# Decay-attention and two feed-forward blocks on one core: input blocks as one 112-row transfer, values on two queues, other planner constants

## The chip, the cores and the metric

One core of a Trainium2 chip runs the whole program. The metric is device time in microseconds; lower is better. The engines are TensorE (PE, with its weight loads PEld), VectorE (DVE), ScalarE (ACT), GpSimd (POOL) and SyncE (SP). TensorE's clock is granted at one of two levels, 2.4 GHz (1.00 in the profile) or 1.2 GHz (0.50).

## The reference

Batch 4, 8 heads, 768 steps, head dimension 48; the 3072 rows of 384 that come out go through two feed-forward blocks.

```python
for t in range(S):                       # attention with a decaying state
    cur = u * k[t] outer v[t]
    y[t] = r[t] @ (state + cur)
    state = w[t] * state + k[t] outer v[t]
x = y as (3072, 384)
x = ((x @ w1) * (x @ w2)) @ w3 @ w_out              # 384 -> 1024 -> 1024 -> 384
out = max(x @ v1, x @ v2, x @ v3) @ v_out           # 384 -> 768 -> 384
```

The weights arrive as 64-bit floats and are converted on the chip.

## The kernel before

**Tiling.** The sequence of each pair of heads is cut into units of 384 steps (`T`), each of six chunks of 64 (`NC`, `C`). There are eight units (`NU`) and in each unit four tiles j (`NJ`) of two heads; the two heads of a tile stand at partitions 0 to 47 and 64 to 111 (`PR` = 112).

**Attention of a unit** (`plan_unit`). For each tile, SyncE loads the block `dm` (L303): decays, reversed keys, receptances, 1159 floats a row. It is loaded in two halves of 48 rows; the rows between them are set once by six memsets in `att_tiles` (L258 to L261). VectorE makes two scans over it, `sf` (L345) and `e` (L352); GpSimd makes the scaled keys `kk` (L356) and receptances `x1`, `x2` (L370, L372). From a second block `tok` (L312) GpSimd makes r*k*u (L314, L316), whose sums per step are the diagonal, `diag`: on ScalarE for unit 1 (L327, `DIAG_ACT`), on VectorE for the others (L329). TensorE makes query-key products (L392), transposes (L398) and chunk states (L459); the states are chained over the chunks by `chain` (L475, L476), on GpSimd for units 0 and 1 (`ON_POOL`), on VectorE for the others. The output product `y` (L417) uses values that were loaded in two halves to `TA` and `TB` (L445, L446). ScalarE and VectorE copy it out as two parts (`yh` L427, `yl` L428), and `xp` (L435) moves a part of it to other partitions by DMA.

**Weights.** Blocks of `wo` (3), `w3` (8) and `w12` (8) are loaded (L758) and converted by VectorE in three passes (L784, L787, L790). W = w3 @ w_out is multiplied out once on TensorE (L826): block i needs w3's block i and all of `wo`. `w12` is split into high and low parts (L817, L818).

**Feed-forward.** For each unit and each of eight slices, A (L509 into `rot`), its product with VectorE (L852), a split (L854, L856), and B with W. After all units, the second feed-forward block runs over the eight units and writes the output.

**The order.** `Plan` holds every step with its engine, cost, needs, claims of buffers and due time. `schedule` runs a list schedule over that model and issues the steps in the resulting order; each engine, and each queue of DMA issues, then runs its steps in that order. A step's urgency is its latest start, worked back from due times. DMAs are modelled as one stream: bytes over `RATE`, plus `LAND`. The due times come from `T_A` (first A), `UNIT` (length of a unit), `T_W` and `D_W` (product of W's block i: T_W + D_W * i), `LEAD` (how far ahead of its first A a unit's attention is due) and `T_V`. Steps with `lock` keep VectorE and GpSimd apart in the model.

```python
add(("dm", *k), "SP", 1.0, load, after=last, size=96 * DMW * 4, ...)
add(("wmul", i, q), "PE", 2.73, w_mul, ..., due=self.T_W + self.D_W * (i + 0.5 * q))
self.due = {"x": lambda u: tA(u * FT) - (min(self.LEAD[1] + self.LEAD[2] * (u - 1), self.LEAD[3]) if u else self.LEAD[0])}
```

Of the kernel before, what the change touches and what calls it, by code (L numbers as in the profile page):

```python
# [9 lines left out]
F32 = mybir.dt.float32  # L10
# [11 lines left out]
B, H, S, D = 4, 8, 768, 48  # L22
NU = 8
T = 384
C = 64
NC = T // C
NJ = 4
DM, FF, FF2 = 384, 1024, 768
KT, FT, MT = DM // 128, FF // 128, FF2 // 128
PR = 112  # L30
NW = NC * (C + 1) + 1
O_K, O_R = NW, NW + T
DMW = NW + 2 * T
# [14 lines left out]
class Plan:  # L48
# [162 lines left out]
class Net:  # L211
# [4 lines left out]
    def constants(self, pool):  # L216
        nc = self.nc
        self.first = pool.tile([PR, NC, C + 1], F32, name="first")
        nc.vector.memset(self.first, 0.0)
        nc.vector.memset(self.first[:, :, 0:1], 1.0)  # L220
        self.inv = [pool.tile([PR, NC, C + 1], F32, name=f"inv{i}") for i in range(2)]
        for t in self.inv:
            nc.gpsimd.memset(t, 0.0)
        self.ident = pool.tile([128, 128], F32, name="ident")
        nc.gpsimd.memset(self.ident, 0.0)
        nc.gpsimd.affine_select(out=self.ident, in_=self.ident, pattern=[[-1, 128]], base=0,
                                channel_multiplier=1, compare_op=ALU.not_equal, fill=1.0)
# [12 lines left out]
        self.wjunk = pool.tile([PR, NW + 1], BF16, name="wjunk")  # L240
        self.il = pool.tile([PR, NU, NJ, NC], F32, name="il")
        self.ub = pool.tile([128, NJ, D], F32, name="ub")

    def att_tiles(self):

        nc, t = self.nc, lambda name, shape, n=1, dt=F32: [self.ap.tile(shape, dt, name=f"{name}{i}") for i in range(n)]
        self.dm, self.tok = t("dm", [PR, DMW], 2), t("tok", [128, 2, NC, D], 2)
        self.e, self.sf = t("e", [PR, NC, C + 1], 2), t("sf", [PR, NC, C + 1], 2)
        self.kk = t("kk", [PR, T], 2)
        self.x1, self.x2 = t("x1", [PR, NC, C], self.NX), t("x2", [128, NC, C], self.NX)  # L250
        self.kt, (self.y,) = t("kt", [128, NC // 2, PR], 2), t("y", [PR, 2, T], 1, F32R)
        self.cd = t("c", [128, NC], 2)
        self.V2, = t("V2", [128, NC // 2, NJ, 2 * D])
        self.TA, = t("TA", [PR, NC * NJ * D])
        self.TB, = t("TB", [128, NC * NJ * D])
        self.U, = t("U", [PR, NC, NJ, D])
        self.fin, = t("fin", [PR, NJ, D])
        for dm in self.dm:  # L258
            nc.vector.memset(dm[32:64, 0:O_K], 1.0)
            nc.vector.memset(dm[32:64, 0:O_K - 1].rearrange("p (c t) -> p c t", t=C + 1)[:, :, 0:1], 0.0)  # L260
            nc.vector.memset(dm[32:64, O_K - 1:], 0.0)  # L261

    NX = 4
    DIAG_ACT = (1,)

    ON_POOL = {"chain": (0, 1), "l": ()}

    def on(self, what, u, dve, pool):
        return ("POOL", pool) if u in self.ON_POOL[what] else ("DVE", dve)
# [4 lines left out]
    def plan_unit(self, u):  # L274

        nc, a, P = self.nc, self.a, self.plan
# [8 lines left out]
        for j in range(NJ):  # L285
# [3 lines left out]
            def dm(k=k):  # L289
                return self.dm[slot["dm", *k][0]]  # L290
# [7 lines left out]
            def bwd(k=k):  # L298
                return dm(k)[0:PR, O_K - 1:0:-1]

            def load(k=k):
                for h in (0, 1):
                    nc.sync.dma_start(dm(k)[64 * h:64 * h + D], a["dm"][k[0], k[1], D * h:D * h + D])  # L303

            add(("dm", *k), "SP", 1.0, load, after=last, size=96 * DMW * 4,
                claims=[("dm", [(w, *k) for w in ("sf", "e", "x1", "x2", "kk", "wchk0", "wchk1")])])
            lt = [("tok", u, j - 1)] if j else [("tok", u - 1, NJ - 1)] if u else []

            def tok(k=k):
                return self.tok[slot["tok", *k][0]]  # L310

            add(("tok", *k), "SP", 0.55, lambda k=k: nc.sync.dma_start(tok(k), a["tok"][k]), after=lt,  # L312
                size=128 * 2 * NC * D * 4, claims=[("tok", [("diag", *k)])])
            add(("rk", *k), "POOL", 0.80, lambda k=k: G.tensor_mul(tok(k)[:, 0], tok(k)[:, 0], tok(k)[:, 1]),  # L314
                [("tok", *k)], lock=True)
            add(("rku", *k), "POOL", 0.80, lambda k=k: G.tensor_mul(  # L316
                tok(k)[:, 0], tok(k)[:, 0], self.ub[:, k[1], :].unsqueeze(1).to_broadcast([128, NC, D])),
                [("rk", *k)], lock=True)

            def cd(k=k):  # L320
                return self.cd[slot["diag", *k][0]]

            def diag(k=k):
                if k[0] in self.DIAG_ACT:
                    for c in range(NC):
                        t = tok(k)[:, 0, c]
                        SC.activation(out=t, in_=t, func=AF.Copy, accum_out=cd(k)[:, c:c + 1])  # L327
                else:
                    V.tensor_reduce(out=cd(k), in_=tok(k)[:, 0], axis=AX.X, op=ALU.add)  # L329

            add(("diag", *k), *(("ACT", 1.6) if u in self.DIAG_ACT else ("DVE", 0.45)), diag,
                [("rku", *k)], claims=[("c", [("dg0", *k), ("dg1", *k)])])

            def sf(k=k):
                return self.sf[slot["sf", *k][0]]
# [28 lines left out]
                return self.x2[slot["x2", *k][0]]  # L364

            def r(k, p, q):
                return dm(k)[p:q, O_R:].rearrange("p (c t) -> p c t", t=C)
# [57 lines left out]
            add(("y", *k), "PE", 0.5, y, [("v1", u), ("s0", u, 0), ("s0", u, 1), *[("s1", u, i) for i in range(4)], ("qk0", *k), ("qk1", *k)] +  # L425
                ([("Ab", 8 * u - 9)] * (u > 1) if j < KT else [("xp", u - 1, j)] * (u > 0)), claims=[("ab", [("yl", *k)])], kind="s")
            add(("yh", *k), "ACT", 0.48, lambda k=k, yt=yt: SC.copy(yt(0), bank(("y", *k))[0:PR, 0:T]), [("y", *k)])  # L427
            add(("yl", *k), "DVE", 0.555, lambda k=k, yt=yt: V.tensor_sub(yt(1), bank(("y", *k))[0:PR, 0:T], f32(yt(0))),  # L428
# [599 lines left out]
def layout(inputs):  # L1028
# [7 lines left out]
    we = np.zeros((NU, NJ, 2, D, NC * (C + 1) + 1), np.float32)
    kd = np.zeros((NU, NJ, 2, D, NC, C), np.float32)
    rd = np.zeros((NU, NJ, 2, D, NC, C), np.float32)
    for i, h in enumerate((1, 0)):
        def rows(x):  # L1040
            return x[:, :, h].transpose(0, 1, 4, 2, 3)
        we[:, :, i, :, :-1].reshape(NU, NJ, D, NC, C + 1)[..., 1:] = rows(W)
        kd[:, :, i] = rows(K)[..., ::-1, ::-1]
        rd[:, :, i] = rows(R)
    dm = np.concatenate([x.reshape(NU, NJ, 2 * D, -1) for x in (we, kd, rd)], axis=3)
# [19 lines left out]
    res |= {"dm": dm, "tok": tok, "v1": v1, "v2": v2, "u": ub, "w3": w3, "wo": wo, "w12": w12}  # L1065
# [21 lines left out]
```

## Time and profile before

| | |
|---|---|
| Median of 3 runs | 771.3 us (770.09 to 771.99) |
| Profiled execution, its own time | 770.51 us |
| Its span, first to last instruction | 768.7 us |
| Mean granted TensorE clock | 0.983 |
| Busy: PE, DVE, ACT, POOL | 737.4, 447.0, 332.9, 243.5 us |

The time of the profiled execution is 1.8 us more than its span. Durations below come from this one execution. A busy TensorE at the low clock level does half the work, so busy time and granted clock are read together. A group's line number is that of the kernel; the feed-forward products have one line, that of a helper (L509).

### The profile page before, as it was taken

To read this page: it belongs to the slowest core of one execution; us is meant where nothing else is said; L and a number is where in the kernel's file an instruction comes from. 1 tells how busy PE (TensorE), PEld (TensorE's weight loads), DVE (VectorE), ACT (ScalarE), POOL (GpSimd) and SP (SyncE) were. 2 spreads that over 40 slices of the span, in tenths; PEclk is the share of its full clock that TensorE was granted. 3 is DMA by queue.
4 is the path that set the end of the run, shared out by engine and by line. 5 is a ranking of instruction groups with operands and counts; after the bars stand their busy time and mean duration, and the time that the engine had idled before them with its cause. 6 is when DMAs were issued, how large, how long until landed. Compare 5 with 4: busy or idle time off the path is not lost.

```text
span 768.7 us, 14960 instructions
## 1 busy us (share of the span) xinstructions
PE 737.4 (96%) x5994; PEld 696.9 (91%) x5994; DVE 447.0 (58%) x731; ACT 332.9 (43%) x798; POOL 243.5 (32%) x293
## 2 busy tenths in 40 slices
PE   3499999999999999999999999999999999999996
PEld 1366788999999999999999999999999999999996
DVE  7798999677876777585547887323232323232222
ACT  2244556354635445354343335667766422222211
POOL 4484678655575565545002332000000000000000
PEclk8689999999999999999999999999999999999999
DMA  7988753445354543344024447576767200000001
GB/s 252 308 274 251 218 185 85 109 110 151 98 139 126 126 93 111 92 125 93 2 82 172 129 159 280 197 256 204 245 204 242 76 32 1 32 1 32 1 31 35
DMA packets 30588, 102.94 MB, mean 134 GB/s; under 512 B 4272, under 2 KB 7472, under 8 KB 30512
## 3 DMA queue, kind: packets, MB, share of 16 engines
q1 hardware_dynamic: 30368, 101.72, 43.2%
q8 instruction: 49, 0.80, 0.4%
q14 instruction: 27, 0.22, 0.1%
q10 hardware_dynamic: 144, 0.20, 0.1%
HBM read 91.28 MB, written 8.26 MB: 129 GB/s over the span
## 4 chain that ended last, share of the span: by engine, by line
PE 93%; DVE 5%; issue 1%; POOL 1%; DMA 0%; ACT 0%; SPq 0%; DVEq 0%; POOLq 0%
PE bank L509 40%; PE rot L509 38%; PE bank L826 6%; PE bank L417 3%; PE bank L392 2%; PE bank L459 1%; PE bank L398 1%; PE bank L393 1%; DVE conv L784 1%; DVE x L405 1%; DMA dm<-in_dm 0%; DVE conv L787 0%; DVE e L352 0%; POOL w L818 0%; DVE gs L856 0%
## 5 line engine op out<-in xcount | busy, mean ns | idle before, releaser
L509 PE MATMUL rot<-xT,w 128*128 128x384 f32 x1152 | 217.2, 339 | 0.9 <-POOL w L818 0.7
L509 PEld LDWEIGHTS rot<-xT,w 128*128 128x128 f32 x1152 | 198.6, 188 | 4.3 <-POOL w L818 1.3
L509 PE MATMUL bank<-x2s,v 128*128 128x384 f32 x684 | 125.6, 336 | 0.0
L509 PEld LDWEIGHTS bank<-x2s,v 128*128 128x128 f32 x684 | 119.0, 188 | 0.0
L509 PE MATMUL bank<-gs,W 128*128 128x384 f32 x576 | 112.6, 338 | 1.2 <-DVE gs L856 1.2
L509 PEld LDWEIGHTS bank<-gs,W 128*128 128x128 f32 x576 | 100.7, 188 | 2.5 <-DVE gs L856 1.8
L956 DVE TENSOR_TENSOR m<-m,bank 128x384 f32<-128x384 f32 x58 | 32.1, 554 | 109.2 <-PE bank L509 99.9
L509 PE MATMUL bank<-vo,ms 128*128 128x384 f32 x432 | 83.5, 337 | 0.0
L509 PE MATMUL rot<-x2s,v 128*128 128x384 f32 x450 | 83.5, 336 | 0.0
L509 PEld LDWEIGHTS rot<-x2s,v 128*128 128x128 f32 x450 | 78.4, 188 | 0.0
L509 PEld LDWEIGHTS bank<-vo,ms 128*128 128x128 f32 x432 | 76.5, 187 | 0.2 <-DVE ms L963 0.2
L961 ACT CAST ms<-m 128x384 fp32r<-128x384 f32 x48 | 24.6, 513 | 96.7 <-DVE m L956 96.4
L850 ACT COPY a<-rot 128x384 f32<-128x384 f32 x64 | 30.6, 478 | 77.6 <-PE rot L509 77.4
L956 DVE TENSOR_TENSOR m<-m,rot 128x384 f32<-128x384 f32 x38 | 21.0, 554 | 66.9 <-PE rot L509 61.0
L854 ACT CAST gs<-g 128x384 fp32r<-128x384 f32 x64 | 32.9, 515 | 61.9 <-DVE g L852 60.3
L852 DVE TENSOR_TENSOR g<-a,rot 128x384 f32<-128x384 f32 x64 | 35.3, 551 | 41.4 <-PE rot L509 40.9
L356 POOL TENSOR_TENSOR kk<-dm,sf 112x384 f32<-112x384 f32 x32 | 32.0, 1006 | 62.3 <-PE bank L393 26.7
L405 DVE COPY_PREDICATED x<-later,bank 64x384 f32<-64x384 uint32 x64 | 37.9, 592 | 22.8 <-PE bank L393 21.8
L826 PE MATMUL bank<-wo,piece 128*128 128x384 f32 x128 | 46.9, 525 | 3.4 <-DVE piece L790 3.4
L856 DVE TENSOR_TENSOR gs<-g,gs 128x384 fp32r<-128x384 f32 x64 | 41.0, 642 | 15.0 <-ACT gs L854 14.8
L370 POOL TENSOR_TENSOR x<-dm,e 48x384 f32<-48x384 f32 x32 | 30.9, 966 | 44.5 <-DVE e L352 27.1
L826 PEld LDWEIGHTS bank<-wo,piece 128*128 128x128 f32 x128 | 25.7, 206 | 21.0 <-DVE piece L790 3.5
(117 smaller groups left out, 1080.1 us busy)
## 6 DMA issues: line engine op xcount, KB each, us to landing
dm<-in_dm SPq DMA_DIRECT2D x64, 217.3 KB, 4.1
tok<-in_tok SPq DMA_DIRECT2D x32, 288.0 KB, 4.0
wst<-in_w SPq DMA_DIRECT2D x8, 1024.0 KB, 8.7
top<-in_w SPq DMA_DIRECT2D x8, 1024.0 KB, 5.0
vst<-in_moe_w SPq DMA_DIRECT2D x9, 768.0 KB, 4.7
top<-in_moe_w SPq DMA_DIRECT2D x9, 768.0 KB, 4.4
wst<-in_w SPq DMA_DIRECT2D x8, 768.0 KB, 5.2
top<-in_w SPq DMA_DIRECT2D x8, 768.0 KB, 4.2
```

The costliest lines, as they stand in the source:

```text
L356: add(("kk", *k), "POOL", 0.86, lambda k=k: G.tensor_mul(kk(k).rearrange("p (c t) -> p c t", t=C), dm(k)[0:PR, O_K:O_R].rearrange("p (c t) ...
L370: add(("x1", *k), "POOL", 0.94, lambda k=k: G.tensor_mul(x1(k)[64:PR], r(k, 64, PR), e(k)[64:PR, :, 0:C]), [("e", *k)], after=lx, lock=Tru ...
L405: add((f"qk{i}", *k), "DVE", 0.59, lambda k=k, x=x, p=p: V.copy_predicated(x(k)[p:p + 64], self.later.bitcast(U32)[p:p + 64].unsqueeze(1). ...
L417: nc.tensor.matmul(ps[0:48, s], self.TA[:, o], x1(k)[:, c, :], start=True, stop=True)
L509: r = self.nc.tensor.matmul(ps, w[p], x[q], start=first and i == 0, stop=last and i == 2)
L826: nc.tensor.matmul(ps[:, 0:DM], t[:, jt * 128:(jt + 1) * 128], wo[:, jt * DM:jt * DM + DM], start=jt == 0, stop=jt == FT - 1)
L850: add(("a", g), "ACT", 0.48, lambda g=g: SC.copy(at[slot["a", g][0]], rot[slot["Aa", g][0]][:, 0:T]), [("Aa", g)], claims=[("a", [("m", g)])])
L852: add(("m", g), "DVE", 0.555, lambda g=g: V.tensor_mul(gt[slot["m", g][0]], at[slot["a", g][0]], rot[slot["Ab", g][0]][:, 0:T]), [("a", g) ...
L854: add(("h", g), "ACT", 0.51, lambda g=g: SC.copy(gst[slot["h", g][0]][:, 0], gt[slot["m", g][0]]), [("m", g)], claims=[("gs", [("B", g)])])
L856: add(("l", g), *self.on("l", u, 0.56, 0.95), lambda g=g, u=u: self.eng("l", u).tensor_sub(gst[slot["h", g][0]][:, 1], gt[slot["m", g][0]] ...
L956: V.tensor_max(t, t, p)
L961: add(("mh", h), "ACT", 0.51, lambda h=h: SC.copy(p2["ms"][slot["mh", h][0]][:, 0], p2["m1"][slot["mx", h, 0][0]]), [("mx", h, 2)], claims ...
```

## The change

The block `dm` becomes one transfer of 112 rows: its rows are padded to 1184 floats, and the rows between the two heads come from memory with it (ones and zeros laid out by the host), so the six memsets go. Of the values, `TA` stays on SyncE's queue and `TB` goes to ScalarE's. The table `ub` (and a small new one, `uf`, which nothing reads with the constants given) is loaded through ScalarE's queue. The diagonal of unit 1 moves from ScalarE to VectorE (the new branch for TensorE is switched off: `DIAG_PE` is empty). The chain of unit 1 moves from GpSimd to VectorE, those of units 3 and 5 from VectorE to GpSimd. The planner gets other constants, and its order follows from them.

```diff
-DMW = NW + 2 * T
+DMW = (NW + 2 * T + 31) // 32 * 32
-    RATE = 285e3
-    LAND = 3.0
+    RATE = 390e3
+    LAND = 2.4
-        for dm in self.dm:
-            nc.vector.memset(dm[32:64, 0:O_K], 1.0)
-            nc.vector.memset(dm[32:64, 0:O_K - 1].rearrange("p (c t) -> p c t", t=C + 1)[:, :, 0:1], 0.0)
-            nc.vector.memset(dm[32:64, O_K - 1:], 0.0)
-    DIAG_ACT = (1,)
-    ON_POOL = {"chain": (0, 1), "l": ()}
+    DIAG_PE = ()
+    ON_POOL = {"chain": (0, 3, 5), "l": ()}
-            def load(k=k):
-                for h in (0, 1):
-                    nc.sync.dma_start(dm(k)[64 * h:64 * h + D], a["dm"][k[0], k[1], D * h:D * h + D])
-            add(("dm", *k), "SP", 1.0, load, after=last, size=96 * DMW * 4, ...)
+            add(("dm", *k), "SP", 0.5, lambda k=k: nc.sync.dma_start(dm(k), a["dm"][k]), after=last, size=128 * DMW * 4, ...)
-                add(("xp", *k), "SP", 2.6, xp, ..., size=96 * 2 * T * 4)
+                add(("xp", *k), "SP", 3.7, xp, ..., size=128 * 2 * T * 4)
-        def v1():
-            nc.sync.dma_start(self.TA[0:64], a["v1"][u, 0:64])
-            nc.sync.dma_start(self.TB[64:128], a["v1"][u, 64:128])
-        add(("v1", u), "SP", 1.1, v1, [("y", u - 1, j) for j in range(NJ)] if u else [], size=128 * NC * NJ * D * 4)
+        for i, (t, p, queue) in enumerate(((self.TA, 0, nc.sync), (self.TB, 64, nc.scalar))):
+            add(("v1", u, i), ("SP", "ACT")[i], 0.55, lambda t=t, p=p, queue=queue: queue.dma_start(t[p:p + 64], a["v1"][u, p:p + 64]),
+                [("y", u - 1, j) for j in range(NJ)] if u else [], size=64 * NC * NJ * D * 4)
-    T_A, UNIT, T_W, D_W, LEAD, T_V = 29.5, 37.7, 18.9, 2.0, (1.0, 16.9, 3.6, 35.2), 20.0
+    T_A, UNIT, T_W, D_W, LEAD, T_V = 22.2, 34.6, 11.0, 5.2, (0, 15.4, 5.1, 35.2), 19.0
-        nc.sync.dma_start(self.ub, a["u"])
+        nc.scalar.dma_start(self.uf, a["uf"])
+        nc.scalar.dma_start(self.ub, a["u"])
```

## Rows read from the trace of the kernel before

**Rows 1.** The page: TensorE's busy time and share; its busy tenths in 40 slices.

```profile
PE 737.4 (96%) x5994; PEld 696.9 (91%) x5994; DVE 447.0 (58%) x731; ACT 332.9 (43%) x798; POOL 243.5 (32%) x293
PE   3499999999999999999999999999999999999996
```

**Rows 2.** Stretches: length, busy time by engine (instructions), granted clock, DMA share, GB/s.

```profile
0.00:40.00 40.00, 17.24 (x127) 10.11 (x128) 30.65 (x42) 9.54 (x27) 19.21 (x32) 0.73 0.91 276
...
80.00:134.00 54.00, 52.09 (x561) 46.12 (x560) 50.75 (x91) 30.43 (x80) 41.15 (x50) 1.00 0.52 155
134.00:760.00 626.00, 625.31 (x5001) 613.94 (x5001) 327.87 (x555) 275.26 (x619) 157.24 (x175) 1.00 0.38 115
```

**Rows 3.** TensorE's waits: whom for, us in total, times, longest.

```profile
PE bank L398 <- POOL kk L356: 11.1, 3, 5.4
PE bank L459 <- DMA V<-in_v: 4.8, 1, 4.8
```

**Rows 4.** Timeline of the start: start us, us, engine, line, operation, count.

```profile
0.82 0.40 SPq L743 DMA_DIRECT2D ub<-in_u  x1
...
3.38 0.70 DVE L261 MEMSET dm<- 32x769 f32 x1
...
4.11 2.12 SPq L303 DMA_DIRECT2D dm<-in_dm  x4
...
8.43 0.97 DVE L345 TENSOR_TENSOR_SCAN sf<-dm,first 112x390 f32<-112x390 f32 x1 [3.01 <-DMA dm<-in_dm]
```

**Rows 5.** Stretches in which halves, weight blocks, and halves again are loaded.

```profile
4.50:8.30 3.80, 3.78 (x6) 1.24 (x4) 0.76 (x2) 0.00 (x0) 0.00 (x0) 1.00 0.87 198
...
11.00:20.00 9.00, 0.83 (x4) 0.50 (x4) 8.69 (x10) 2.40 (x10) 5.52 (x5) 0.54 1.02 407
21.50:26.00 4.50, 1.12 (x3) 0.79 (x3) 4.01 (x5) 0.70 (x2) 3.03 (x6) 0.50 1.03 207
```

**Rows 6.** DMA issues before 20 us: size of each, median us to landing.

```profile
dm<-in_dm SPq DMA_DIRECT2D x7, 217.3 KB, 4.9
...
TA<-in_v SPq DMA_DIRECT2D x1, 288.0 KB, 13.3
```

**Rows 7.** Timeline of VectorE: two instructions after idle time.

```profile
26.88 0.97 DVE L345 TENSOR_TENSOR_SCAN sf<-dm,first 112x390 f32<-112x390 f32 x1 [1.30 <-DMA dm<-in_dm]
...
30.67 1.20 DVE L405 COPY_PREDICATED x<-later,bank 64x384 f32<-64x384 uint32 x2 [2.59 <-PE bank L393]
```

**Rows 8.** W's blocks: timelines of TensorE and VectorE, and the chain's longest piece.

```profile
24.91 4.76 PE L826 MATMUL bank<-wo,piece 128*128 128x384 f32 x8 [3.38 <-DVE piece L790]
...
50.92 5.43 PE L826 MATMUL bank<-wo,piece 128*128 128x384 f32 x16
...
75.94 1.20 DVE L784 TENSOR_SCALAR conv<-wst 128x1024 uint32<-128x1024 uint32 x1
...
78.50 1.22 DVE L790 SCALAR_TENSOR_TENSOR piece<-wst,conv 128x1024 uint32<-128x1024 uint32 x1
...
65.29 20.84 PE bank L826 x64
```

**Rows 9.** Diagonals and chain steps on VectorE (ns min/median/max); scans during unit 1's chain (us, mean ns).

```profile
L329 DVE TENSOR_REDUCE c<-tok x28: 417/447/455, 24.8 to 351.7; 128x6 f32<-128x288 f32 x28
...
L475 DVE TENSOR_TENSOR U<-U,il x30: 333/359/897, 159.9 to 385.9; 112x192 f32<-112x192 f32 x30
...
L476 DVE TENSOR_TENSOR U<-U x30: 357/358/851, 160.2 to 386.3; 112x192 f32<-112x192 f32 x30
...
L345 DVE TENSOR_TENSOR_SCAN sf<-dm,first 112x390 f32<-112x390 f32 x2 | 4.3, 2139 | 0.0
```

**Rows 10.** SyncE's queue, its own waits: us in total, times, longest.

```profile
SPq L445 <- PE bank L418: 23.5, 7, 7.7
```

More of the change, by code (lines that the diff above doesn't have):

```diff
@@ L242, in constants @@
         self.ub = pool.tile([128, NJ, D], F32, name="ub")
+        self.uf = pool.tile([PR, NJ], F32, name="uf")
     def att_tiles(self):
@@ L299, in bwd @@
                 return dm(k)[0:PR, O_K - 1:0:-1]
-            def load(k=k):
-                for h in (0, 1):
-                    nc.sync.dma_start(dm(k)[64 * h:64 * h + D], a["dm"][k[0], k[1], D * h:D * h + D])
-            add(("dm", *k), "SP", 1.0, load, after=last, size=96 * DMW * 4,
-                claims=[("dm", [(w, *k) for w in ("sf", "e", "x1", "x2", "kk", "wchk0", "wchk1")])])
-            lt = [("tok", u, j - 1)] if j else [("tok", u - 1, NJ - 1)] if u else []
+            add(("dm", *k), "SP", 0.5, lambda k=k: nc.sync.dma_start(dm(k), a["dm"][k]), after=last, size=128 * DMW * 4,
+                claims=[("dm", [(w, *k) for w in ("sf", "e", "x1", "x2", "kk", "wchk0", "wchk1") + ("rk",) * (u in self.DIAG_PE)])])
@@ L309, in tok, with first @@
+            def first(u):
+                return "rk" if u in self.DIAG_PE else "tok"
+            lt = [(first(u), u, j - 1)] if j else [(first(u - 1), u - 1, NJ - 1)] if u else []
             def tok(k=k):
                 return self.tok[slot["tok", *k][0]]
[L312 to L315, printed above, removed]
@@ L316, in plan_unit @@
-            add(("rku", *k), "POOL", 0.80, lambda k=k: G.tensor_mul(
-                tok(k)[:, 0], tok(k)[:, 0], self.ub[:, k[1], :].unsqueeze(1).to_broadcast([128, NC, D])),
-                [("rk", *k)], lock=True)
             def cd(k=k):
                 return self.cd[slot["diag", *k][0]]
-            def diag(k=k):
-                if k[0] in self.DIAG_ACT:
-                    for c in range(NC):
[L326 to L329, printed above, removed]
@@ L331, in plan_unit, with rk, dp @@
-            add(("diag", *k), *(("ACT", 1.6) if u in self.DIAG_ACT else ("DVE", 0.45)), diag,
-                [("rku", *k)], claims=[("c", [("dg0", *k), ("dg1", *k)])])
+            if u in self.DIAG_PE:
+                def rk(k=k):
+                    return self.tok[slot["rk", *k][0]].rearrange("p a c d -> p (a c d)")[0:PR, 0:T]
+                add(("rk", *k), "POOL", 0.95, lambda k=k: G.tensor_mul(
+                    rk(k), dm(k)[0:PR, O_K:O_R], dm(k)[0:PR, O_R + T - 1:O_R - 1:-1]), [("dm", *k)], after=lt, lock=True,
+                    claims=[("tok", [("dp", *k)])])
+                def dp(k=k):
+                    ps = self.ab[slot["dp", *k][0]]
+                    for c in range(NC):
+                        q = slice(T - c * C - C, T - c * C)
+                        nc.tensor.matmul(ps[0:64, c:c + 1], rk(k)[64:PR, q], self.uf[64:PR, k[1]:k[1] + 1], start=True, stop=True)
+                        nc.tensor.matmul(ps[64:128, c:c + 1], rk(k)[0:48, q], self.uf[0:48, k[1]:k[1] + 1], start=True, stop=True)
+                add(("dp", *k), "PE", 0.35, dp, [("rk", *k)], claims=[("ab", [("diag", *k)])], kind="s")
+                add(("diag", *k), "ACT", 0.2, lambda k=k: SC.copy(cd(k), self.ab[slot["dp", *k][0]][:, 0:NC]), [("dp", *k)],
+                    claims=[("c", [("dg0", *k), ("dg1", *k)])])
+            else:
+                add(("tok", *k), "SP", 0.55, lambda k=k: nc.sync.dma_start(tok(k), a["tok"][k]), after=lt,
+                    size=128 * 2 * NC * D * 4, claims=[("tok", [("diag", *k)])])
+                add(("rk", *k), "POOL", 0.80, lambda k=k: G.tensor_mul(tok(k)[:, 0], tok(k)[:, 0], tok(k)[:, 1]),
+                    [("tok", *k)], lock=True)
+                add(("rku", *k), "POOL", 0.80, lambda k=k: G.tensor_mul(
+                    tok(k)[:, 0], tok(k)[:, 0], self.ub[:, k[1], :].unsqueeze(1).to_broadcast([128, NC, D])),
+                    [("rk", *k)], lock=True)
+                add(("diag", *k), "DVE", 0.45, lambda k=k: V.tensor_reduce(out=cd(k), in_=tok(k)[:, 0], axis=AX.X, op=ALU.add),
+                    [("rku", *k)], claims=[("c", [("dg0", *k), ("dg1", *k)])])
@@ L366, in r @@
             def r(k, p, q):
-                return dm(k)[p:q, O_R:].rearrange("p (c t) -> p c t", t=C)
+                return dm(k)[p:q, O_R:O_R + T].rearrange("p (c t) -> p c t", t=C)
             lx = [("x1", u, j - 1)] if j else [("x1", u - 1, NJ - 1)] if u else []
@@ L423, in yt @@
                 return t[:, i]
-            add(("y", *k), "PE", 0.5, y, [("v1", u), ("s0", u, 0), ("s0", u, 1), *[("s1", u, i) for i in range(4)], ("qk0", *k), ("qk1", *k)] +
+            add(("y", *k), "PE", 0.5, y, [("v1", u, 0), ("v1", u, 1), ("s0", u, 0), ("s0", u, 1), *[("s1", u, i) for i in range(4)], ("qk0", *k), ("qk1", *k)] +
                 ([("Ab", 8 * u - 9)] * (u > 1) if j < KT else [("xp", u - 1, j)] * (u > 0)), claims=[("ab", [("yl", *k)])], kind="s")
@@ L437, in plan_unit @@
             if j == KT:
-                add(("xp", *k), "SP", 2.6, xp, [("yl", u, i) for i in range(NJ)] + [("Ab", 8 * u - 9)] * (u > 1), size=96 * 2 * T * 4)
+                add(("xp", *k), "SP", 3.7, xp, [("yl", u, i) for i in range(NJ)] + [("Ab", 8 * u - 9)] * (u > 1), size=128 * 2 * T * 4)
         nd = NJ * D
@@ L1034, in layout @@
     R, K, V, W = units(r), units(k), units(v), units(w)
[L1036 to L1039, printed above, removed]
+    dm = np.zeros((NU, NJ, PR, DMW), np.float32)
+    we = dm[..., 0:O_K - 1].reshape(NU, NJ, PR, NC, C + 1)
+    we[..., 1:] = 1
+    kd, rd = (np.zeros((NU, NJ, PR, NC, C), np.float32) for _ in range(2))
+    for h, p in ((1, 0), (0, 64)):
         def rows(x):
             return x[:, :, h].transpose(0, 1, 4, 2, 3)
[L1042 to L1045, printed above, removed]
+        we[:, :, p:p + D, :, 1:] = rows(W)
+        kd[:, :, p:p + D] = rows(K)[..., ::-1, ::-1]
+        rd[:, :, p:p + D] = rows(R)
+    dm[..., 0:O_K - 1] = we.reshape(NU, NJ, PR, -1)
+    dm[..., O_K:O_R] = kd.reshape(NU, NJ, PR, -1)
+    dm[..., O_R:O_R + T] = rd.reshape(NU, NJ, PR, -1)
+    uf = np.zeros((PR, NJ), np.float32)
+    for h, p in ((1, 0), (0, 64)):
+        uf[p:p + D] = u.reshape(NJ, 2, D)[:, h].T
     tok = np.stack([R[:, :, :, :, ::-1], K[:, :, :, :, ::-1]], axis=2)
@@ L1064, in layout @@
     res["u2"] = u2
-    res |= {"dm": dm, "tok": tok, "v1": v1, "v2": v2, "u": ub, "w3": w3, "wo": wo, "w12": w12}
+    res |= {"dm": dm, "tok": tok, "v1": v1, "v2": v2, "u": ub, "w3": w3, "wo": wo, "w12": w12, "uf": uf}
     for n in ("moe_w1", "moe_w2", "moe2_w1", "moe2_w2", "moe2_w3", "moe2_w_out"):
```

## The prediction

> **What bounds the kernel now.** I first read the busy shares and the forty slices. TensorE is busy 96% of the span, and the only slices under nine tenths are the first two and the last [rows 1]. Nearly all that can be won lies in the first 40 us; the last slice is the drain of the output, which the change doesn't touch.
>
> Next, four stretches. In the first 40 us TensorE works 17.24 us, so it idles 22.8 us, and at a mean granted clock of 0.73; VectorE works 30.65 us of the 40 and the DMA engines are busy 0.91 of them. From 80 to 134 us TensorE idles 1.9 us and VectorE works 50.75 of 54. From 134 to 760 us TensorE idles 0.7 us of 626 [rows 2]. So past 134 us the time is a sum of matmuls that no edit changes; the span is that sum plus whatever TensorE lost before.
>
> Who makes it lose? Its waits name the key products (GpSimd) and the state values (a DMA) [rows 3], but those wait for VectorE and the transfers themselves. The W blocks show how tight it is: the three passes that convert the last w3 block run on VectorE from 75.94 to 79.72 us, and TensorE's last four products of W run without a break from 65.29 to 86.13 us at some 5.4 us a block [rows 8], so the last starts near 80.7, 1 us after its block is converted. TensorE looks full from 40 us on, but it is fed just in time. VectorE's work up to about 134 us is the bound, and each microsecond by which it runs earlier is one off the span.
>
> **The change part by part.**
>
> *Memsets and the first block.* Before, SyncE's first issue is the table of u at 0.82 us; the first block of decays, keys and receptances is issued at 4.11 us, right after the memset of its tile ends (3.38 + 0.70), and the first scan starts at 8.43 us [rows 4]. After, no memset writes that tile and u's table is on ScalarE's queue, so the block is SyncE's first issue, at about 0.82: 3.3 us earlier. VectorE has nothing but memsets in those 6 us, and the removed memsets themselves sit inside that wait, so they count nothing beyond it. ScalarE has no instruction before 8.43 us, so its two small issues cost it nothing; without that cover they would cost some 0.4 us each, like u's issue on SyncE [rows 4].
>
> *One transfer of 112 rows.* A block was two halves of 217.3 KB, 445 KB in all, each into one side of the partitions [rows 6]. While only such halves travel (also the value halves TA and TB) the DMA engines are fully busy, yet move 198 and 207 GB/s; while the 128-row weight blocks travel they move 407 [rows 5]. The new block is 112 x 1184 x 4 = 530 KB. At 407 it takes 1.3 us against 2.2 before, 0.9 less; at 207 it would take 2.6, 0.4 more. I take 407, since the new form is nearest to the whole-height blocks, and keep the other end. The Trainium skill (SBUF — State Buffer, Door 1: The DMA port swizzle) says that partitions 0 to 63 reach only half of the ports, which fits the halves' rate. The first scan then starts near 8.43 - 3.3 - 0.9 = 4.2 us: **4.2 us gained**, 2.9 at the bad end.
>
> *Less time in the queue.* Later blocks are 0.9 us shorter too, and everything queued behind them lands sooner. Before 40 us VectorE idles 1.3 us for a block, at 26.88, and 2.6 us for the query-key products at 30.67 [rows 7]. The first wait should go: the engine would need it about as late as before and the queue is 4 us ahead. The second is a wait for TensorE, which ran the eight matmuls before it at half its speed, 4.76 us where sixteen take 5.43 later [rows 8]. I take half, between nothing and all. Together **2.6 us gained**, bounds 0 to 3.9.
>
> *Values by two queues.* ScalarE's queue gets one issue per unit, waiting for the last output product of the unit before; queued behind it are ScalarE's copies out of PSUM. SyncE's same wait sums to 23.5 us over seven, 7.7 at most [rows 10]. But ScalarE copies that same product out anyway, so its trigger waits where the copy waits: nothing, or 7.7 us once if the list puts it before other work. The values need to be there only when the first output products run, after the matmuls at 50.92 us [rows 8], and were issued at about 10 and landed some 13.3 us later [rows 6]: hidden. If both halves overlap they go at 407 instead of 207, 1.4 us less for 590 KB. Against this stands a rule of the Trainium skill (SBUF — State Buffer, "Can I just issue two DMAs to hit both halves?"): two at once into the two halves measured 6% over one. No row here shows it; the sum would be the same by both, as I count the values at nothing.
>
> *Unit 1's work comes to VectorE.* Its four diagonal sums move from ScalarE to VectorE: 4 x 0.447 = 1.8 us. Its six chain steps move from GpSimd: 6 x (0.359 + 0.358) = 4.3 us. In exchange, during the chain on GpSimd two scans took 4.3 us where the plain one takes 0.97 [rows 4, 9], so 2.3 us come back if they were slowed by GpSimd. Net 3.8 us of VectorE [rows 9] between 58 and 134 us, where it has only 3.25 us free in the last 54 [rows 2]. I take half as late, **1.9 us lost**, bounds 0 and 6.1. Units 3 and 5 go the other way; they lie past 134 us, where TensorE is never short, so they count nothing; a stall there would cost at most those 4.3 us each.
>
> *The order.* The new rates and due times make the planner list the work anew. Relative to unit 0's first use, blocks 2 to 5 of w3 become less urgent (before, block i leads by 9.6 - 2i, after by 11.2 - 5.2i). I count that at nothing while VectorE has no gaps, as it does the same work in any order; the rival below is what it costs otherwise.
>
> *Sum:* 4.2 + 2.6 - 1.9 = 4.9 us. The profiled execution took 770.5 us (span 768.7); it becomes 765.6. The median of the runs shown is 0.8 us above it: **766.4 us**.
>
> **The rivals.**
>
> *The order starves TensorE (slower).* If VectorE takes attention ahead of w3 blocks, TensorE waits up to 3.8 us per block, the three passes [rows 8], since attention feeds it little. Three blocks put back: 766.4 + 11.3 = 777.7 us. It decides once fewer than two blocks have run on TensorE by 50 us while it still idles. For it: the due times above. Against: much of attention waits for GpSimd, and VectorE fills such gaps with w3.
>
> *Given back at unit 1 (no change).* All 6.1 us of moved work is late and only the first block is faster: 771.3 - 4.2 - 1.3 + 6.1 = 771.9 us. For it: VectorE at 94% there. Against: the slowed scans.
>
> *More than the waits.* The 2.6 us wait goes whole, nothing is lost at unit 1, TensorE's 1.9 us idle there goes [rows 2]: 4.2 + 3.9 + 1.9 = 10 us, 761.3. The half-speed matmuls (4.76 us where half of 5.43 would do) could add 2.0 us, 759.3.
>
> *The 112 rows go no faster than the halves.* Then only the earlier issue counts: 2.9 + 1.3 - 1.9 = 2.3 us, 769.
>
> **How the numbers follow.** Forecast 0.45, more than the waits 0.15, no faster rows 0.10 (half of it within the bound), given back 0.16, starved 0.14. About 0.3%, or 2.3 us, is what a measurement here can tell: faster 0.66, same 0.20, slower 0.14. The range runs from a little below the best case, 758.5, to a little above the given-back one, 772.5; it leaves out most of the starved case and the tip of the best.
>
> **What would show it.** The first scan near 4.2 us, and the first product of W near 20 instead of 24.91. Stretches with only the new blocks near 400 GB/s. TensorE's idle before 40 us down from 22.8 to about 17. From 80 to 134 us VectorE fuller, TensorE's idle near 2 us. Past 134 us nothing. I am wrong if the first scan moves and TensorE's idle before 80 us doesn't shrink (order), or if the idle reappears between 80 and 134 us (unit 1).

## The result and the profile after

The changed kernel takes 782.4 us in the median of four runs (779.95 to 785.16), the kernel before 771.6 us in runs beside it: a ratio of 1.0144, 95% interval 1.0104 to 1.0184. It is 11 us slower where I forecast 5 us faster. The profiled execution took 785.2 us, the longest of the four; its span is 783.5 us against 768.7, at a mean granted clock of 0.972 against 0.983.

First the stretches of the changed kernel (columns as in [rows 2]); the last line is the stretch of the kernel before that [rows 2] leaves out.

```profile
0.00:40.00 40.00, 19.85 (x162) 11.59 (x166) 29.93 (x38) 10.13 (x28) 20.68 (x35) 0.74 0.95 311
40.00:80.00 40.00, 38.38 (x273) 23.92 (x266) 33.45 (x43) 11.64 (x28) 19.04 (x27) 0.92 0.75 223
80.00:134.00 54.00, 46.65 (x388) 39.75 (x389) 49.35 (x84) 23.60 (x58) 34.11 (x38) 0.87 0.49 157
134.00:783.00 649.00, 642.30 (x5193) 628.56 (x5189) 331.86 (x555) 283.32 (x636) 187.98 (x206) 1.00 0.37 117
...
40.00:80.00 40.00, 40.00 (x296) 24.54 (x295) 36.56 (x44) 16.19 (x71) 25.87 (x37) 0.97 0.87 270
```

Before 40 us TensorE idles 20.2 us, 2.6 less than in [rows 2]. Then the profit turns into a loss: from 80 to 134 us it idles 7.35 us where it idled 1.9, and its clock, 1.00 before, is 0.87. So 642.3 us of its work is left at 134 us. Before, it was 737.4 us in all less 109.3 in the first 134, 628.1. Those 14.2 us are nearly the whole 14.8 us of the span. Idle time explains 4.4 of them (29.1 us in the first 134 against 24.7). The other 9.8 us are matmuls that ran longer for the same work, as the busy time shows: 747.2 us against 737.4, for 5994 matmuls in both. The clock accounts for most of them: 2.8% of 783.5 us is missing, against 1.7% of 768.7, which is 8.9 us. That is an upper bound, as it counts slow stretches in which TensorE idled too; where it was busy at the low level the clock records give 7.4 us. The remaining 2.4 us are not explained.

Where it waits is in the timelines (start, length, instruction, in brackets the idle time before it and what ended it). The start:

```profile
5.55 0.97 DVE L352 TENSOR_TENSOR_SCAN sf<-dm,first 112x390 f32<-112x390 f32 x1 [2.91 <-DMA dm<-in_dm]
...
12.35 1.23 DVE L791 TENSOR_SCALAR conv<-wst 128x1024 uint32<-128x1024 uint32 x1 [1.56 <-DMA wst<-in_wo]
...
24.44 0.97 DVE L352 TENSOR_TENSOR_SCAN sf<-dm,first 112x390 f32<-112x390 f32 x1 [1.74 <-DMA dm<-in_dm]
25.44 0.20 DVE L357 RECIPROCAL inv<-sf 112x6 f32<-112x6 f32 x1
25.55 1.18 DVE L797 SCALAR_TENSOR_TENSOR piece<-wst,conv 128x1024 uint32<-128x1024 uint32 x1
...
26.79 5.49 PE L833 MATMUL bank<-wo,piece 128*128 128x384 f32 x8 [11.35 <-DVE piece L797]
```

The first scan is 2.9 us earlier than in [rows 4]. Yet the first product of W comes at 26.79, 1.9 us later than in [rows 8]: VectorE waits 1.56 us for `wo`, and the third pass of w3's first block (25.55) stands behind a scan whose block lands at 24.3. The pass itself had all it needed when the one before it ended at 22.7. TensorE meanwhile idles 11.35 us.

At the end of W's products:

```profile
77.02 0.56 DVE L791 TENSOR_SCALAR bank<-wst 128x384 uint32<-128x384 uint32 x1 [2.50 <-DMA wst<-in_w]
...
82.14 1.22 DVE L797 SCALAR_TENSOR_TENSOR piece<-wst,conv 128x1024 uint32<-128x1024 uint32 x1
...
83.46 2.99 PE L515 MATMUL rot<-xT,w 128*128 128x384 f32 x9 [2.52 <-issue]
```

VectorE waits 2.5 us for a w12 block, with the last w3 block queued behind it; that one is converted at 83.4 us instead of 79.7 [rows 8]. TensorE starts again 0.1 us later, after 2.5 us of nothing. The profile names no releaser, but the program does: its step `conv` waits for all three passes of every `wo` and w3 block and only then gives `rot`, into which this matmul writes, its PSUM banks.

And at unit 1's chain:

```profile
122.82 0.56 DVE L797 SCALAR_TENSOR_TENSOR part<-wst,bank 128x384 uint32<-128x384 uint32 x1
...
123.97 0.62 PE L515 MATMUL rot<-xT,w 128*128 128x384 f32 x2 [2.25 <-ACT w L824]
124.14 1.07 DVE L482 TENSOR_TENSOR U<-U 112x192 f32<-112x192 f32 x1
...
125.05 6.73 PE L515 MATMUL rot<-xT,w 128*128 128x384 f32 x18 [0.47 <-POOL w L825]
```

TensorE waits for a w12 part that VectorE finished at 123.4 between the chain's steps. The 18 matmuls after that take 6.73 us; 18 of the same line take 3.12 us at the high level (137.47 us in the kernel before). The rows of that stretch and of the one ahead of it say why; the two lines above them are an earlier pair, and the last is from the kernel before:

```profile
105.00:110.00 5.00, 3.44 (x84) 2.78 (x82) 3.79 (x7) 2.36 (x6) 3.69 (x5) 1.00 0.79 266
110.00:115.00 5.00, 4.71 (x62) 4.37 (x60) 4.83 (x8) 2.99 (x9) 4.69 (x6) 0.66 0.59 175
...
120.00:125.00 5.00, 2.34 (x14) 1.77 (x12) 4.76 (x9) 1.94 (x5) 2.06 (x4) 0.97 0.05 18
125.00:130.00 5.00, 4.87 (x13) 3.99 (x14) 4.72 (x10) 2.81 (x8) 1.88 (x2) 0.50 0.22 59
...
115.00:120.00 5.00, 3.82 (x46) 3.25 (x46) 4.92 (x8) 4.03 (x10) 4.61 (x8) 1.00 0.49 157
```

A granted clock of 0.50 is the 1.2 GHz level: 4.87 of 5.00 us are busy, at half the work. In the 5 us before, the engine had worked 2.34 us. The shorter gaps between 105 and 110 us are followed by a clock of 0.66 in the same way; the kernel before idled 1.2 us in one stretch, 115 to 120 us, and kept 1.00. So an idle gap can be paid twice, once as idle and once more as slow matmuls behind it.

### The profile page after: what moved, and what is told of

Same layout as the page of the kernel before. It is cut to its first block, busy times and chain, and to the rows that moved or that the text cites. A ratio compares the mean times of both kernels' runs of the same rounds, so it can differ in the third digit from the quotient of the medians.

```text
span 783.5 us, 14815 instructions
## 1 busy us (share of the span) xinstructions
PE 747.2 (95%) x5994; PEld 703.8 (90%) x5994; DVE 444.6 (57%) x717; ACT 328.7 (42%) x750; POOL 261.8 (33%) x305
## 4 chain that ended last, share of the span: by engine, by line
PE 89%; DMA 5%; DVE 3%; issue 1%; ACT 1%; POOL 0%; SPq 0%; ACTq 0%; DVEq 0%
PE bank L515 40%; PE rot L515 37%; PE bank L833 3%; PE bank L424 3%; DMA dm<-in_dm 2%; PE bank L399 2%; PE bank L465 1%; DMA wst<-in_w 1%; DMA TB<-in_v 1%; PE bank L405 1%; PE bank L400 1%; DVE x L412 1%; DVE U L481 0%; DVE U L482 0%; PE bank L425 0%
## 5 line engine op out<-in xcount | busy, mean ns | idle before, releaser
L515 PE MATMUL rot<-xT,w 128*128 128x384 f32 x1152 | 223.3, 344 | 6.6 <-issue 2.5
L515 PEld LDWEIGHTS rot<-xT,w 128*128 128x128 f32 x1152 | 203.2, 191 | 12.2 <-issue 3.1
L515 PE MATMUL rot<-x2s,v 128*128 128x384 f32 x450 | 83.5, 335 | 0.0
L382 ACT ACTIVATE wjunk<-dm,bias 112x391 bf16<-112x391 f32 x64 | 40.0, 625 | 26.2 <-DMA dm<-in_dm 25.5
L352 DVE TENSOR_TENSOR_SCAN sf<-dm,first 112x390 f32<-112x390 f32 x32 | 38.7, 1211 | 17.9 <-DMA dm<-in_dm 17.9
```

What stands on the lines that cost most here:

```text
L352: add(("sf", *k), "DVE", 0.97, lambda k=k: V.tensor_tensor_scan(out=sf(k).rearrange("p c t -> p (c t)"), data0=bwd(k), data1=self.first.re ...
L382: add((f"wchk{i}", *k), "ACT", 0.81, lambda k=k, i=i, sc=sc: SC.activation(out=self.wjunk[:, 0:NW], in_=we(k), func=AF.Relu, bias=self.bia ...
L515: r = self.nc.tensor.matmul(ps, w[p], x[q], start=first and i == 0, stop=last and i == 2)
```

## The experiments

Every kernel below computes the whole reference; what differs is how blocks are moved, where steps run and in which order. The time of before beside them was 770.6 to 771.0 us.

**Movement and order apart.** The change is two things: other transfers, and another list (with unit 1's and two more units' work on other engines). One kernel has the new transfers (one block of 112 rows, no memsets, u's table and `TB` on ScalarE's queue) in the order of before, step for step; the next the same with `TB` left on SyncE; the third has the order of after with the old transfers.

```diff
 e1, from before:
...
+                nc.sync.dma_start(dm(k), a["dm"][k])
-            add(("dm", *k), "SP", 1.0, load, after=last, size=96 * DMW * 4,
+            add(("dm", *k), "SP", 1.0, load, after=last, size=96 * 1159 * 4,
...
+            nc.scalar.dma_start(self.TB[64:128], a["v1"][u, 64:128])
...
 e2, from e1:
-            nc.scalar.dma_start(self.TB[64:128], a["v1"][u, 64:128])
+            nc.sync.dma_start(self.TB[64:128], a["v1"][u, 64:128])
 e3, from after:
+                for p in (0, 64):
+                    nc.sync.dma_start(dm(k)[p:p + D], a["dm"][k][p:p + D])
...
```

> The order of every engine is that of the kernel before; only the data movement is new: one 112-row transfer per block, no memsets, the table of u and the TB half on ScalarE's queue. Theory A (the new order is what costs, the movement itself helps): the first scan starts near 5.5 us, TensorE's idle before 40 us falls by some 3 us, time 766 to 769 us. Theory B (the movement costs: a 112-row transfer or the half on ScalarE's queue slows the stream): 775 us or more. Theory C (the movement is hidden, the order is all): 771 us.

> As the first run, but TB stays on SyncE's queue behind TA. If the TB half that starts beside the first block slows that block, the first scan starts some 0.7 us earlier than with TB on ScalarE's queue, near 4.8 us, and the time is 0 to 1 us lower; if two halves on two queues overlap usefully, it is later in landing both and 0 to 1 us slower.

> The order of every engine is that of the changed kernel; the data movement is the old one (two halves per block, memsets, everything on SyncE's queue). Theory A (order costs): 783 to 790 us, as slow as the changed kernel or slower by the 3 us of the later first block. Theory B (movement costs): near 772 us.

| | old transfers | new transfers |
|---|---|---|
| order of before | 771.0 | e1 769.1 (ratio 0.9979 [0.9967, 0.9990]); e2 768.6 (0.9964 [0.9951, 0.9977]) |
| order of after | e3 784.4 (1.0192 [1.0150, 1.0235]) | after 782.4 (1.0144 [1.0104, 1.0184]) |

Read along the first row: the new transfers gain 2 us. In the order of after the medians differ by 2 us as well, but the intervals overlap. Read down a column: the order, with the moved work in it, loses 13 us with either transfers. That settles which part made the kernel slower; in the traces of e1 and e2 VectorE (but for the memsets), ScalarE and GpSimd run before's instructions in before's order. The intervals of e1 and e2 overlap: the second queue gives nothing that these runs show.

Why 2 and not 7 us? In e2, the stretch in which the first new blocks travel, and three steps:

```profile
4.00:7.00 3.00, 3.00 (x7) 1.42 (x5) 0.81 (x1) 0.83 (x1) 0.00 (x0) 1.00 1.03 264
...
6.19 0.97 DVE L339 TENSOR_TENSOR_SCAN sf<-dm,first 112x390 f32<-112x390 f32 x1 [3.56 <-DMA dm<-in_dm]
...
28.60 1.21 DVE L399 COPY_PREDICATED x<-later,bank 64x384 f32<-64x384 uint32 x2 [3.96 <-PE bank L387]
...
22.68 4.92 PE L820 MATMUL bank<-wo,piece 128*128 128x384 f32 x8 [4.11 <-DVE piece L784]
```

112 rows move at 264 GB/s, not 407: at that rate 530 KB take 2.0 us. (Weight rows join them in the last microsecond; 4 to 6 us alone gives 269.) The first scan starts 2.2 us earlier, the first product of W 2.2 us earlier, and the span is 2.3 us shorter (766.4). The block wait of [rows 7] is gone, but the wait for the query-key products behind it grew from 2.59 to 3.96 us. VectorE only waits in another place, since the list still makes it wait for TensorE there.

**Rows of a whole height.** If 112 rows are slow and 128 are fast, a block padded with 16 rows of zeros should win though it is 14% larger.

```diff
 e12, from e2:
+PD = 128
...
-        self.dm, self.tok = t("dm", [PR, DMW], 2), ...
+        self.dm, self.tok = t("dm", [PD, DMW], 2), ...
...
```

> The old order with the new transfers, TB on SyncE's queue (768.6 us); the block is padded to 128 rows (606 KB instead of 530). If 112 rows run at some 265 GB/s because they don't fill the sixteen engines and partitions evenly, 128 rows run near 400: 1.5 us a block instead of 2.0, the first scan starts 0.4 to 0.6 us earlier than 6.2, the time is 0 to 1 us lower. If the rate is one of the long odd rows, it stays near 265 GB/s, the first scan is 0.3 us later and the time the same or higher.

766.8 us (766.51 to 767.40), ratio 0.9950 [0.9934, 0.9967], 4 us below the kernel before and the fastest median of this study. Its interval overlaps that of e2, so what the 16 rows give is read from the trace. Same stretch and steps:

```profile
4.00:7.00 3.00, 3.00 (x6) 1.47 (x5) 1.64 (x3) 1.79 (x2) 0.66 (x1) 1.00 1.02 416
...
5.23 0.97 DVE L340 TENSOR_TENSOR_SCAN sf<-dm,first 112x390 f32<-112x390 f32 x1 [2.60 <-DMA dm<-in_dm]
...
21.72 4.51 PE L821 MATMUL bank<-wo,piece 128*128 128x384 f32 x8 [4.32 <-DVE piece L785]
```

416 GB/s (417 from 4 to 6 us, before weight rows are most of it), so at that rate 606 KB take 1.5 us where 530 KB took 2.0. Scan and first W product are each 0.96 us earlier than in e2, and the span is 765.2, 1.2 us shorter.

**Unit 1's work at a fixed order.** In e8 the order is that of e2, only unit 1's chain and diagonal are carried out by VectorE in the same places of the list. In e7 the order is that of after, with unit 1's chain carried out by GpSimd and its diagonal by ScalarE.

```diff
 e8, from e2:
-        return self.nc.gpsimd if u in self.ON_POOL[what] else self.nc.vector
+        return self.nc.gpsimd if u in self.ON_POOL[what] and (what, u) != ("chain", 1) else self.nc.vector
...
-                if k[0] in self.DIAG_ACT:
+                if False:
 e7, from after:
+        return self.nc.gpsimd if u in self.ON_POOL[what] or (what, u) == ("chain", 1) else self.nc.vector
...
+                    if k[0] == 1:
...
```

> The order of the kernel before with the new transfers (TB on SyncE's queue, 768.6 us); only unit 1's chain and diagonal sums are carried out on VectorE at their old places in the order. Theory U: 6.1 us more on VectorE, 2 to 6 us slower, 771 to 775 us, with TensorE idle between 105 and 125 us. If the engine doesn't matter: 768 to 769 us.

> The order of the changed kernel, step for step; only unit 1's chain is carried out on GpSimd and its diagonal sums on ScalarE, at the places that the order has for them. Theory U: the idle between 105 and 135 us shrinks by 4 us or more and the time is 774 to 778 us. Theory D or P (the place of the chain in the order, not the engine, is late): 780 us or more.

e8: 772.6 us (1.0023 [1.0012, 1.0034]), 4.0 more than e2. e7: 779.6 (1.0108 [1.0087, 1.0128]), 2.8 less than after. So the move costs some 4 us by itself in the order of before; in that of after the 2.8 us lie within the intervals. In e8 it shows as one gap of TensorE behind VectorE's queue:

```profile
118.17 2.93 PE L503 MATMUL bank<-gs,W 128*128 128x384 f32 x8 [4.04 <-DVE gs L850]
...
117.56 0.55 DVE L850 TENSOR_TENSOR gs<-g,gs 128x384 fp32r<-128x384 f32 x1
...
118.69 0.96 DVE L339 TENSOR_TENSOR_SCAN sf<-dm,first 112x390 f32<-112x390 f32 x1
```

The same wait is 0.5 us in e2. The two scans there take 0.96 and 0.93 us, but in e2, with the chain on GpSimd, they took 1.36 and 0.99: what comes back is 0.5 us, not 2.3.

**Constants put back, planned anew.** Each of these is after with one or more of its planner's inputs as before, and the list made again. e4 has the old `RATE` and `LAND`, e6 the old due times, e5 unit 1's work as before, e9 the last two, e10 the old rates and unit 1, e11 all three.

```diff
 e4, e10, e11:
-    RATE = 390e3
-    LAND = 2.4
+    RATE = 285e3
+    LAND = 3.0
 e6, e9, e11:
-    T_A, UNIT, T_W, D_W, LEAD, T_V = 22.2, 34.6, 11.0, 5.2, (0, 15.4, 5.1, 35.2), 19.0
+    T_A, UNIT, T_W, D_W, LEAD, T_V = 29.5, 37.7, 18.9, 2.0, (1.0, 16.9, 3.6, 35.2), 20.0
 e5, e9, e10, e11 (with the branch of `diag` for ScalarE):
-    ON_POOL = {"chain": (0, 3, 5), "l": ()}
+    DIAG_ACT = (1,)
+    ON_POOL = {"chain": (0, 1), "l": ()}
...
```

> The changed kernel, with the planner's DMA rate and landing time of before (285 KB/us and 3.0 us instead of 390 and 2.4); a new order follows. Theory A1 (optimistic DMA times put steps ahead that then wait in an in-order engine): VectorE's and ScalarE's waits for the blocks and weights before 90 us shrink from some 10 us, and the time falls to 770 to 776 us. Rival A2 (due times or unit 1's work on VectorE make the bad order): 780 to 785 us.

> The changed kernel, with the chains on GpSimd for units 0 and 1 and unit 1's diagonal sums on ScalarE as before; the new rates and due times stay and the planner makes a new order. Theory U (unit 1's 6.1 us of work on VectorE starve TensorE between 80 and 134 us): TensorE's idle there falls from 7.3 us to 2 to 3, its clock there back to 1.00, time 770 to 774 us. Theory D (the due times are the cause): 778 to 784 us, with TensorE's gap near 80 us still there.

> The changed kernel, with the due times of before (first use 29.5, unit 37.7, W 18.9 + 2.0 per block, leads 1.0, 16.9, 3.6); new rates and unit 1's moved work stay, and the planner makes a new order. Theory D: the last w3 block is converted by 77 us and TensorE has no gap between 40 and 90 us, time 769 to 774 us. Theory U: 777 to 783 us, with the loss between 100 and 135 us.

> The changed kernel with the old due times and unit 1's work back on GpSimd and ScalarE; only the DMA rate and landing of the planner are new, beside the transfers. If the losses of due times (2.6 us) and of unit 1's work (7.7 us) add up: 782.4 - 10.3 = 772 us. If the optimistic DMA times cost by themselves, it stays 3 us or more above the 768.6 us of the old order with the new transfers; if they do nothing, it comes to 768 to 770 us.

> The changed kernel with the planner's DMA rates of before and unit 1's work as before; only the due times are new, beside the transfers. If the three losses (rates 2.2, unit 1 7.7, due times 2.6 us) add: 772.5 us. If the due times alone, without gaps behind DMA waits, are harmless: 768 to 770 us.

> The changed kernel with all planner constants and unit 1's work as before: what is new are the transfers, with TB on ScalarE's queue, and their costs in the plan. A theory by which the constants and unit 1 are all of the loss gives 768 to 770 us, as the old order with the new transfers (769.1). If it stays above 772 us, the list is sensitive to the changed costs of the transfers too.

| put back | us | ratio to before |
|---|---|---|
| e4 rates | 780.2 | 1.0124 [1.0099, 1.0150] |
| e6 due times | 779.8 | 1.0107 [1.0087, 1.0128] |
| e5 unit 1 | 774.6 (single runs 771.2 to 779.1) | 1.0074 [1.0044, 1.0103] |
| e9 due times, unit 1 | 776.0 | 1.0080 [1.0062, 1.0097] |
| e10 rates, unit 1 | 778.2 | 1.0096 [1.0079, 1.0112] |
| e11 all three | 779.4 | 1.0114 [1.0095, 1.0134] |

Had the loss been one constant's, one of these would have come near 769 and e11 with it. None does, and the sets don't add up: with unit 1 back the time is 774.6, and with the rates back on top 778.2 (e5's runs spread over 8 us, and these two intervals overlap). In e11 only the transfers' own entries in the plan are new (issue costs, bytes, values as two steps), and it is still 10 us slower than e1, which has the same transfers. My theory that the new due times starve TensorE falls with e6, and the rival that unit 1's move is all of it falls with e7.

**Nudges of the untouched kernel.** If any replanning costs this much, a constant of no importance should do it too. Each of these four is the kernel before, old transfers and all, with one input of its planner nudged, one pair of lines each.

```diff
 one each in e13, e14, e15, e16:
-    LAND = 3.0
+    LAND = 2.9
-    HOP = 0.12
+    HOP = 0.13
-    RATE = 285e3
+    RATE = 290e3
-            add(("dm", *k), "SP", 1.0, load, ...
+            add(("dm", *k), "SP", 0.9, load, ...
```

> The kernel before, untouched but for one planner constant: DMA landing time 2.9 us instead of 3.0. No transfer and no work changes; only the order does. Theory S (the order of before is a picked one, and nearly any new list order costs 4 to 10 us because engines run in order and the plan's times are not the chip's): 774 to 781 us. Theory C (the changed kernel's own constants are bad, a neutral nudge is harmless): 770 to 772 us.

> The kernel before with the planner's delay from one engine to another at 0.13 us instead of 0.12, nothing else. Theory S: 774 to 781 us, theory C: 770 to 772 us.

> The kernel before with the planner's DMA rate at 290 KB/us instead of 285, nothing else. Theory S: 774 to 781 us, theory C: 770 to 772 us.

> The kernel before with the planner's cost for issuing a block at 0.9 us instead of 1.0 (the changed kernel says 0.5), nothing else. Theory S: 772 to 781 us, with fewer steps moved than in the other three perhaps at the lower end. Theory C: 770 to 772 us.

| nudge | us | ratio to before |
|---|---|---|
| e16 issue cost 1.0 to 0.9 | 771.0 | 1.0003 [0.9993, 1.0013] |
| e13 `LAND` 3.0 to 2.9 | 772.3 | 1.0016 [1.0005, 1.0027] |
| e15 `RATE` 285e3 to 290e3 | 773.9 | 1.0047 [1.0029, 1.0065] |
| e14 `HOP` 0.12 to 0.13 | 779.4 | 1.0104 [1.0085, 1.0122] |

None is faster, and ten nanoseconds on the planner's allowance for a hand-over between engines (`HOP`) cost 8.4 us, by the pattern seen in after. The four differ in where their lists depart from before's. On VectorE, ScalarE and GpSimd the first instruction out of before's order stands at 185.1 us in e16 and at 172.9 in e13; in e15 it stands at 50.7 and in e14 at 44.5. So e16 and e13 left the first 134 us as they were and cost 0 and 1 us; the two that moved steps there cost 3.0 and 8.4. The first 134 us of before, e16, e13, e15 and e14:

```profile
0.00:134.00 134.00, 109.34 (x981) 80.77 (x981) 117.96 (x175) 56.16 (x177) 86.22 (x119) 0.91 0.74 226
...
0.00:134.00 134.00, 109.11 (x981) 80.66 (x981) 118.28 (x175) 56.13 (x177) 86.41 (x119) 0.91 0.75 226
...
0.00:134.00 134.00, 109.30 (x981) 80.78 (x981) 118.54 (x175) 55.82 (x177) 86.14 (x119) 0.91 0.73 226
...
0.00:134.00 134.00, 107.04 (x916) 78.59 (x917) 113.81 (x170) 54.75 (x172) 82.73 (x117) 0.90 0.74 224
...
0.00:134.00 134.00, 103.70 (x883) 73.53 (x884) 111.25 (x161) 52.30 (x166) 81.21 (x112) 0.86 0.72 219
```

From e14, two of its stretches and TensorE's longest new wait (whom for, us in total, times, longest):

```profile
40.00:80.00 40.00, 38.84 (x334) 23.65 (x332) 33.79 (x39) 17.18 (x76) 27.88 (x38) 0.95 0.81 246
80.00:134.00 54.00, 47.87 (x426) 39.87 (x426) 47.25 (x81) 25.59 (x65) 34.84 (x43) 0.94 0.53 157
...
PE bank L826 <- DVE W L831: 5.0, 1, 5.0
```

TensorE waits 5.0 us for a PSUM bank that VectorE has to empty into W, a step that the list put late; the last matmul of W starts at 99.5 us instead of 85.6, and the clock is 0.95 and 0.94 where it was 0.97 and 1.00.

## Why the prediction was wrong

**The step that failed** is "*The order* ... I count that at nothing while VectorE has no gaps, as it does the same work in any order". It cost 13 us with the moved work in it (e1 to after, e2 to after 14; before to e3 13), and about 10 without: e7, the order of after with unit 1's work on its old engines, takes 779.6 us against e1's 769.1. The premise was wrong twice. VectorE does have gaps in after: it works 112.7 us of the first 134 against 118.0 before, since its queue stops at `wo`, at a block and at a w12 load while work that is ready stands behind. And "the same work in any order" looks at the wrong engine: what counts is when TensorE is fed, and an engine fed just in time can lose twice by a gap.

**The starved rival** had the sign and a size in reach (777.7 against 782.4), and 0.14 was far too little. Its mechanism was only half right. Its point of decision, fewer than two blocks by 50 us, did not come: eight matmuls of W run at 26.79 and eight more by 36.7, then twenty-four from 42.52, at sixteen a block. The gaps came at other places: up to 26.8, 42.5, 83.5 and 124 us, and smaller ones between 105 and 110. Its price had no slow matmuls in it, which turned out to be two thirds of the profiled execution's loss. Nor are the due times its cause (e6).

**Memsets and the first block**, 4.2 us with 2.9 at the bad end: the earlier issue came (SyncE issues at 0.82), the first scan moved 2.2 to 2.9 us (e2, after). The term that was mis-sized is the rate. I took 407 GB/s for 112 rows because they are "nearest to the whole-height blocks"; they moved at 264 to 266, nearer to the halves' 198 to 207 of [rows 5]. Of the heights tried, only 128 gives 416. The Trainium skill (DMA: Bandwidth & Descriptors, Rules for kernel authors) asks for one transfer of 128 partitions in place of two halves; e12 agrees, with 416 GB/s against 198 for the halves.

**Less time in the queue**, 2.6 us: nothing. In e2 the gain of the first scan, 2.2 us, is already that of the whole kernel, 2.3; the block wait went, but moved into the wait for TensorE behind it.

**Values by two queues**, nothing: right. e1 and e2 are alike. Either way the values were not what anything late waited for, so no run here shows whether two halves at once gain the 6% that the Trainium skill's rule quoted there gives. `TB` landed 8.2 us after its issue in e1 and 9.9 in after, beside SyncE's blocks.

**Unit 1's work**, 1.9 us lost with bounds 0 and 6.1: 4.0 at the order of before, 2.8 (within the noise) at that of after. The sign and the bounds held; "I take half as late" was low, by two terms. The twelve chain steps, counted at 4.3 us from [rows 9], take 5.9 us on VectorE in e8 and 8.0 in after (these rows of after: busy us, mean ns):

```profile
L482 DVE TENSOR_TENSOR U<-U 112x192 f32<-112x192 f32 x5 | 3.5, 700 | 0.2
L481 DVE TENSOR_TENSOR U<-U,il 112x192 f32<-112x192 f32 x5 | 3.3, 669 | 0.0
L481 DVE TENSOR_TENSOR fin<-fin,il 112x192 f32<-112x192 f32 x1 | 0.7, 654 | 0.0
L482 DVE TENSOR_TENSOR U<-U,fin 112x192 f32<-112x192 f32 x1 | 0.5, 496 | 0.1
```

[rows 9] has 897 ns as the longest of such a step beside a median of 359; I took the median. And of the 2.3 us that I let the scans give back, 0.5 came (e8). My reading of [rows 9] was wrong there: the longer of the two scans ran after the chain. In the kernel before,

```profile
118.80 3.00 DVE L345 TENSOR_TENSOR_SCAN sf<-dm,first 112x390 f32<-112x390 f32 x1
...
117.91 1.14 POOL L476 TENSOR_TENSOR U<-U 112x192 f32<-112x192 f32 x1
119.01 1.96 POOL L818 TENSOR_TENSOR w<-part,w 128x384 fp32r<-128x384 f32 x2
```

the chain's last step ends at 119.05, and the scan's 3.00 us lie almost wholly behind it, beside GpSimd's work on w12 and then the keys, which stays on GpSimd when the chain moves. Units 3 and 5 cost nothing, as forecast: past 134 us TensorE idles 7.2 us in after and 6.7 in before, the drain among them.

**The signs to look for** did their work: "wrong if the first scan moves and TensorE's idle before 80 us doesn't shrink (order), or if the idle reappears between 80 and 134 us (unit 1)". The first scan moved; idle before 80 us shrank by 1.0 us only (21.8 against 22.8), and 5.4 us reappeared later. (The forecast's chances add up to 0.65 for faster and 0.21 for the same, not to 0.66 and 0.20; nothing hangs on it.)

**What stays open.** Which of the moved steps of the list cost how much is not settled. By the runs, unit 1's move is worth 3 to 4 of the 13 us; the rest goes with no single constant. Nine lists differ from before's in the first 134 us (after, e4 to e6, e9 to e11, e14, e15), and all nine have slower medians, by 3 to 11 us. That before's list is a rare good one, which the planner's model (a DMA stream, fixed costs, no slow clock) cannot tell from the others, is the simplest reading; it was not shown by a larger sample of lists. Nor is the list all: the five runs of e5 share one list and lie between 771.2 and 779.1 us. Its trace is of the fastest, with 24.7 us of idle in the first 134, as before; why the others took longer is not known. And no new list was searched for that suits the new transfers.

## What to carry to other kernels

Where a list scheduler orders a kernel that feeds TensorE just in time, a change of any of its inputs is a new draw of the order: keep the old order fixed while a part of the change is judged, and price the replanning from a few neutral nudges of the kernel before (here 3 and 8 us; two more moved no step in the stretch that counts and cost next to nothing) ahead of any gain of 2 us. A gap on TensorE is to be priced with the slow matmuls behind it: they cost twice the added idle in after (9.8 against 4.4 us), and 4.0 us beside 5.6 of added idle in e14. And a block of nearly whole height is worth a trial at 128 rows: here it moved the first scan and the first product of W forward by 1 us.

## What the hardware showed

- Transfers of 48 rows moved 198 GB/s, with value halves of 64 rows among them 207 [rows 5]; of 112 rows 264 (e2) to 266 (after), of 128 rows 416 (e12). By these rates the padding adds 14% of bytes and takes a quarter off the time.
- Behind gaps that ended at 83.5 us (2.5 us) and 124 us (2.25 us), and behind smaller ones between 105 and 110 us (1.6 us in all), TensorE ran at the 1.2 GHz level for several microseconds, also while nearly fully busy: 0.50 over 125 to 130 us, 4.87 us busy. In all the same matmuls took 9.8 us longer, against 4.4 us of added idle.
- Two scans of 390 elements beside GpSimd's work (the end of unit 1's chain, then w12) took 4.3 us in the kernel before [rows 9] and 2.35 us in e2, in the same order; with the chain on VectorE (e8) 1.89. How much GpSimd slows them thus hangs on what meets what, which no run here takes apart.
